# Retention then a sigmoid-gated FFN on Trainium2: the first token tile loaded and computed in natural layout instead of in halves of two chunks

## The chip, the cores and the metric

One Trainium2 chip, one core of it. The metric is the device time of one execution in microseconds (us); a kernel's time is the median of its runs. The inputs are float32 in device memory, the output is float32.

## What is computed

Recurrent retention over 4 batch entries, 8 heads, 768 tokens and head size 64, and then a gated feed-forward block on the 3072 resulting rows of 512:

```
gamma = 1 - 2 ** (-5 - arange(H))
for t in range(S):
    state = gamma * state + k[:, :, t] (outer) v[:, :, t]
    y[:, :, t] = q[:, :, t] @ state / sqrt(D)
x = y as [B * S, H * D]                      # 3072 x 512
out = (sigmoid(x @ w_gate) * (x @ w_val)) @ w_out   # d_ff = 1536
```

## The kernel before, in words

**Tiling.** The sequence is cut into six tiles of 128 tokens. A tile holds 128 tokens of all four batch entries, which is 512 rows of the FFN. The recurrence is done in its chunked form. Inside a chunk the scores k.q are multiplied by a decay or a causal mask (VectorE) and multiplied with v. What comes from earlier chunks goes through a running state `za`, of which `zb` is the bf16 copy. A tile is two "pairs" i, each of two batch entries j, so pairs 0 and 1 are tile 0, and pairs 2 to 11 are tiles 1 to 5.

**Tiles 1 to 5.** `load_kq` and `load_v` load a pair: k and q by DMAs that cast to bf16 (lines 63 and 67), v in float32 (line 57), all issued by GpSimd (POOL). `scale_v` (line 202) makes `vs`, v times a power of gamma from the table `tabs`, on POOL or on VectorE (DVE). k and q are transposed by TensorE (`transpose`, pairs 2 and 3) or by DMA transposes that SyncE (SP) issues (`xbar`, line 193, pairs 4 to 11). `block(old, new)` then runs the products: `scores` (line 210), `mask` (216), `inter` (226), `intra` (233), `y_out` (241), `state` (248), `state_sum` (257).

**The FFN.** `up(t, n1)` makes one of 12 slices of hidden units: four matmuls with the gate weights and four with the value weights (line 366), a sigmoid on ScalarE (ACT, line 376) and a product on DVE (line 377). `down` (line 393) multiplies with `w_out`, copies out of PSUM on ACT and stores through SP.

**Tile 0** has code of its own. k of pair 0 comes in float32 by two hardware queues (SP and ACT, `k0f`), v of pair 1 in float32 by SP (`v1f`, issued at lines 432-433). q, k of pair 1 and v of pair 0 come by casting DMAs on POOL. Here one batch entry of a pair lies on 64 partitions with two neighbouring tokens each (`k2`, `v2`), and q on 32 partitions with four (`q4`), so that the pieces in device memory are 512 or 1024 bytes long. `first_k`, `first_q`, `first_scores`, `first_y` and `first_state` work on half and quarter arrays (64x64). For the state of tile 0, POOL scales k of pair 0 (`k0s`) and v of pair 1 (`v1s`), line 342. `keep_on(n)` issues n matmuls of the identity (line 420) whose result nobody reads.

**What sets the order.** The program order of each engine is that of the code: `tc.manual_schedule()`. The `plan` at the end says behind which FFN group of tiles 1 to 4 each step of the recurrence stands. POOL's DMA issues share eight semaphores: the ninth waits until the first has landed, and so on.

Of the kernel before, what the change touches and what calls it, by code (L numbers as in the profile page):

```python
# [8 lines left out]
F32 = mybir.dt.float32  # L9
# [6 lines left out]
def kernel(  # L16
# [37 lines left out]
    def load_v(i):  # L54
        t, h = divmod(i, 2)
        vf[i] = ld.tile([C, 2 * H, D], F32, tag="vf", name="vf", bufs=4)
        nc.gpsimd.dma_start(out=vf[i], in_=v[2 * h:2 * h + 2, :, t * C:(t + 1) * C, :].rearrange("b h s d -> s (b h) d"))  # L57
# [33 lines left out]
    def first(t, x, b, n, part, eng):  # L91
        r = C // n
        eng.dma_start(out=t[part * r:(part + 1) * r].rearrange("p h j d -> p h (j d)"),
                      in_=x[b, :, 0:C, :].rearrange("h (p j) d -> p h (j d)", j=n))

    k0f = ld.tile([C, H, 2, D], F32, tag="vf", name="k0f", bufs=4)
    v1f = ld.tile([C, H, 2, D], F32, tag="vf", name="v1f", bufs=4)
    k2 = [ld.tile([C, H, 2, D], BF16, tag="kn", name="k2", bufs=6) for _ in range(2)]
    k0s = ld.tile([C, H, 2, D], BF16, tag="kn", name="k0s", bufs=6)
    q4 = at.tile([C, H, 4, D], BF16, tag="kqX", name="q4", bufs=4)  # L100
    v2 = [at.tile([C, H, 2, D], BF16, tag="vs", name="v2", bufs=4) for _ in range(2)]
    v1s = at.tile([C, H, 2, D], BF16, tag="vs", name="v1s", bufs=4)

    first(k0f, k, 0, 2, 0, nc.sync)
    first(k0f, k, 1, 2, 1, nc.scalar)
    nc.scalar.preload_act_table(AX.Exp)
    tok = const.tile([128, NT + 2], F32, name="tok")
    col = const.tile([128, C], F32, name="col")
    dist = const.tile([128, 2, C], F32, name="dist")
    nc.gpsimd.iota(tok[:, 0:NT], pattern=[[C, NT]], base=0, channel_multiplier=1, allow_small_or_imprecise_dtypes=True)  # L110
    nc.gpsimd.iota(col, pattern=[[1, C]], base=0, channel_multiplier=0, allow_small_or_imprecise_dtypes=True)
    nc.gpsimd.iota(dist, pattern=[[-1, 2], [1, C]], base=0, channel_multiplier=-2, allow_small_or_imprecise_dtypes=True)
    for b in range(B):
        first(q4, q, b, 4, b, nc.gpsimd)


    for b in range(2):
        first(k2[1], k, 2 + b, 2, b, nc.gpsimd)
    for b in range(2):
        first(v2[0], v, b, 2, b, nc.gpsimd)  # L120
    for s in range(2):
        load_gate_val(s)

    lgp = const.tile([128, NP], F32, name="lgp")
    lsc = const.tile([128, 1], F32, name="lsc")
    nlg = const.tile([128, H], F32, name="nlg")
    nc.vector.memset(lsc, math.log(scale))
    for h in range(H):
        nc.vector.memset(lgp[h % 2 * D:(h % 2 + 1) * D, h // 2:h // 2 + 1], lg[h])
    lsn = const.tile([128, NP], F32, name="lsn")  # L130
    nc.vector.tensor_scalar(lsn, lgp, float(C), math.log(scale), op0=ALU.mult, op1=ALU.add)
    ident = const.tile([128, 128], BF16, name="ident")
    causal = const.tile([128, 128], F32, name="causal")
    farther = const.tile([128, 2, C], F32, name="farther")
    nc.vector.tensor_scalar(ident, col, tok[:, 0:1], None, op0=ALU.is_equal)  # L135
    nc.vector.tensor_scalar(dist[D:128], dist[D:128], 2.0 * D, None, op0=ALU.add)
    nc.vector.scalar_tensor_tensor(farther, dist, -1.0e6, dist, op0=ALU.mult, op1=ALU.max)
    nc.vector.tensor_scalar(tok[:, NT:NT + 2], dist[:, :, 0], -1.0, None, op0=ALU.mult)
    for h in range(H):
        nc.vector.memset(nlg[:, h:h + 1], -lg[h])  # L140
    tabs = const.tile([128, H, NT + 2], F32, name="tabs")
    nc.vector.tensor_tensor(tabs, tok.unsqueeze(1).to_broadcast([128, H, NT + 2]),
# [7 lines left out]
    def make_taby1(p):  # L150
        nc.scalar.activation(taby[:, 1, p, :], col, AX.Exp, scale=lgp[:, p:p + 1], bias=lsn[:, p:p + 1])
# [425 lines left out]
```

## Time and profile before

| | us |
|---|---|
| runs of the kernel before | 240.84, 243.07, 243.61 |
| their median | 243.07 |
| the profiled execution | 243.72 |
| its span from first to last instruction | 242.0 |
| TensorE matmul busy | 223.2 (92%) |
| DVE / ACT / POOL busy | 109.2 / 80.0 / 101.6 |

The profile is of one execution. In its rows, a group of instructions has an engine, a line, the operation, what it writes and reads, how often it occurs, and in brackets how long the engine stood idle ahead of it and what ended that. "PE" is TensorE's matmuls, "PEld" its weight loads. The chain of waits follows the work that ended last back to the start. "PEclk" is the granted TensorE clock. In the rows of DMA queues, q0 is what POOL issues and q1 is what SP issues; a size of "128.0 KB" is that of what is written, which for a casting load is half of what is read.

### The profile page before, as it was taken

The page shows a single profiled execution, that of the slowest core. Times are in us where ns is not written, and L with a number is a line of the kernel's source. Part 1 is how long each engine was busy: PE and PEld are TensorE (multiplying, and loading weights), DVE is VectorE, ACT ScalarE, POOL GpSimd, SP SyncE. Part 2 cuts the span into 40 slices and gives each one's busy share as a digit, 9 for nine tenths or more (in the row PEclk, how much of TensorE's full clock was granted, in tenths as well). Part 3 has the DMA queues.
Part 4 walks back from the last instruction along what each step waited for, and adds up shares of the span by engine and source line. Part 5 has one row for each costly group of instructions (what it writes and reads, how often), then busy time and mean ns, then how long its engine had stood idle before and what let it go on. Part 6 is the DMA issues. An engine that isn't in the chain of part 4 may idle for free.

```text
span 242.0 us, 4687 instructions
## 1 busy us (share of the span) xinstructions
PE 223.2 (92%) x1925; PEld 124.4 (51%) x1948; DVE 109.2 (45%) x189; ACT 80.0 (33%) x133; POOL 101.6 (42%) x123
## 2 busy tenths in 40 slices
PE   2892999998959999999999999999999999999995
PEld 1761744454748885454454544544544544444444
DVE  3572145417289345575491454490634651243401
ACT  7543324332522421233332143231233222233211
POOL 8941985889997281399769420000000000000000
PEclk9999599999999999999999999999999999999999
DMA  7999799999999999999999974001150002200022
GB/s 132 183 199 185 87 176 176 215 175 193 249 147 133 98 125 139 106 265 106 180 98 175 253 141 90 0 0 75 58 131 3 0 0 89 88 0 0 3 85 88
DMA packets 77269, 28.09 MB, mean 116 GB/s; under 512 B 61888, under 2 KB 73024, under 8 KB 77248
## 3 DMA queue, kind: packets, MB, share of 16 engines
q0 software_dynamic: 54496, 16.26, 70.9%
q1 hardware_dynamic: 22080, 11.21, 27.6%
q10 hardware_dynamic: 672, 0.33, 0.5%
q8 instruction: 15, 0.25, 0.5%
q14 instruction: 6, 0.05, 0.1%
HBM read 28.31 MB, written 6.29 MB: 143 GB/s over the span
## 4 chain that ended last, share of the span: by engine, by line
PE 86%; DMA 6%; DVE 5%; issue 1%; ACT 0%; SPq 0%; DVEq 0%; ACTq 0%
PE ff L366 52%; PE ff L393 24%; DMA v1f<-in_v_dram 4%; DVE vs L202 2%; PE ff L233 2%; DMA k0f<-in_k_dram 2%; PE ff L210 2%; PE ff L226 1%; PE ff L406 1%; PE ff L248 1%; DVE qT L308 1%; DVE st L216 1%; PE ff L187 1%; PE ff L420 1%; PE ff L334 0%
## 5 line engine op out<-in xcount | busy, mean ns | idle before, releaser
L377 DVE TENSOR_TENSOR hT<-gs,ff 128x512 bf16<-128x512 f32 x72 | 49.0, 686 | 75.3 <-PE ff L366 71.8
L366 PE MATMUL ff<-xT,wg 128*128 128x512 bf16 (+1 forms) x338 | 74.5, 347 | 1.0 <-ACT xT L339 0.6
L366 PE MATMUL ff<-xT,wv 128*128 128x512 bf16 (+1 forms) x340 | 74.9, 350 | 0.1
L376 ACT ACTIVATE gs<-ff 128x512 f32<-128x512 f32 x72 | 42.9, 597 | 78.9 <-PE ff L366 76.7
L393 PE MATMUL ff<-wo,hT 128*128 128x512 bf16 x263 | 61.1, 379 | 0.9 <-issue 0.3
L366 PEld LDWEIGHTS <-wv 128*128 128x128 bf16 x344 | 34.4, 100 | 29.5 <-issue 0.2
L366 PEld LDWEIGHTS <-wg 128*128 128x128 bf16 x344 | 33.4, 99 | 28.7 <-issue 0.7
L393 PEld LDWEIGHTS <-hT 128*128 128x128 bf16 x276 | 26.2, 98 | 30.7
L397 ACT COPY ob<-ff 128x512 f32<-128x512 f32 x23 | 13.4, 585 | 49.3 <-PE ff L393 49.2
L216 DVE TENSOR_TENSOR st<-ff,causal 128x512 bf16<-128x512 f32 x40 | 24.7, 679 | 6.3 <-PE ff L210 6.3
L241 DVE TENSOR_TENSOR xT<-ff,taby 128x512 bf16<-128x512 f32 x20 | 12.9, 686 | 31.2 <-PE ff L233 31.2
L67 POOL DMA_DIRECT2D qn<-in_q_dram x20 | 15.2, 773 | 13.9 <-DMA qn<-in_q_dram 13.4
L202 POOL TENSOR_TENSOR vs<-vf,tabs 128x1024 bf16<-128x1024 f32 x8 | 15.7, 1960 | 4.0 <-DMA vf<-in_v_dram 3.6
L67 POOL DMA_DIRECT2D kn<-in_k_dram x20 | 15.2, 765 | 2.3 <-DMA kn<-in_k_dram 2.2
L57 POOL DMA_DIRECT2D vf<-in_v_dram x10 | 11.9, 1193 | 5.2 <-DMA qn<-in_q_dram 3.4
L261 ACT CAST zb<-za 128x512 bf16<-128x512 f32 x10 | 6.2, 616 | 13.4 <-DVE za L257 12.2
L63 POOL DMA_DIRECT2D kn<-in_k_dram x10 | 9.1, 910 | 1.3 <-DMA vf<-in_v_dram 1.3
L63 POOL DMA_DIRECT2D qn<-in_q_dram x10 | 9.1, 907 | 0.2 <-DMA kn<-in_k_dram 0.2
L420 PE MATMUL ff<-ident 128*128 128x128 bf16 x52 | 6.0, 290 | 2.0 <-DVE ident L135 2.0
L233 PE MATMUL ff<-st,vs 128*64 128x128 bf16 x160 | 6.6, 222 | 0.7 <-DVE vs L202 0.7
L248 PE MATMUL ff<-vs,kn 128*64 128x64 bf16 x128 | 3.6, 196 | 2.7 <-DVE vs L202 2.7
L420 PEld LDWEIGHTS <-ident 128*128 128x128 bf16 x52 | 4.6, 132 | 2.7 <-DVE ident L135 2.0
(74 smaller groups left out, 124.0 us busy)
## 6 DMA issues: line engine op xcount, KB each, us to landing
out_dram<-ob SPq DMA_DIRECT2D x23, 256.0 KB, 2.9
vf<-in_v_dram POOLq DMA_DIRECT2D x10, 512.0 KB, 8.6
wg<-in_moe_w_gate_dram POOLq DMA_DIRECT2D x6, 256.0 KB, 6.7
wv<-in_moe_w_val_dram POOLq DMA_DIRECT2D x6, 256.0 KB, 7.4
wo<-in_moe_w_out_dram POOLq DMA_DIRECT2D x4, 384.0 KB, 8.0
kn<-in_k_dram POOLq DMA_DIRECT2D x10, 128.0 KB, 8.3
kn<-in_k_dram POOLq DMA_DIRECT2D x20, 64.0 KB, 8.5
qn<-in_q_dram POOLq DMA_DIRECT2D x10, 128.0 KB, 9.3
```

The lines of the kernel that those rows point to most:

```text
L57: nc.gpsimd.dma_start(out=vf[i], in_=v[2 * h:2 * h + 2, :, t * C:(t + 1) * C, :].rearrange("b h s d -> s (b h) d"))
L63: nc.gpsimd.dma_start(out=tiles[i][:, 0:H], in_=src[0])
L67: nc.gpsimd.dma_start(out=dst[:, e], in_=pairs[:, 1 - e])
L202: eng.tensor_tensor(vs[i][:, j0 * H:(j0 + n) * H, :].rearrange("s (j h) d -> s j h d", j=n), vf[i][:, j0 * H:(j0 + n) * H, :].rearrange("s ...
L216: nc.vector.tensor_tensor(st[i, j], sc[i, j][e], causal4, op=ALU.mult)
L241: nc.vector.tensor_tensor(xT[t][:, :, c:c + C], y[i, j], taby[:, t], op=ALU.mult)
L366: nc.tensor.matmul(u[:, i * n:(i + 1) * n], w[:, kk, n1 * 128:(n1 + 1) * 128], xT[t][:, kk, lo:hi], start=(kk == 0), stop=(kk == KT - 1))
L376: nc.scalar.activation(g, ps[0], AX.Sigmoid)
L377: nc.vector.tensor_tensor(hT[t][:, n1s[0]:n1s[-1] + 1, lo:hi], g.rearrange("p (i n) -> p i n", n=n), ps[1].rearrange("p (i n) -> p i n", n ...
L393: nc.tensor.matmul(o, hT[t][:, n1, b * C:(b + 1) * C], wo[:, n1, :], start=(n1 == 0), stop=(n1 == NFF - 1))
L397: nc.scalar.copy(ob, o)
L420: nc.tensor.matmul(u[:, :128], ident, ident, start=True, stop=True)
```

## The change

Tile 0 is loaded and computed like the other tiles: 128 tokens on 128 partitions, one batch entry (a "half tile", `entry(t, j)`) after the other. k and q of the very first batch entry come in float32 by SP and ACT and are cast by DVE and ACT. All else of tile 0 comes by casting DMAs on POOL's queue, in the order k, q of entries 1, 2, 3 and then v of both pairs, with pieces of 256 bytes in device memory. v is not scaled for tile 0; the state is made from `ks`, k scaled by POOL in four half tiles (line 309 of the new file), and the decay table for tile 0 is over (token, token) of one entry. The tables that are needed later (`tabs`, `taby`, `causal`) are made behind the first scores. `up` of tile 0 starts with all 512 rows instead of two halves of 256. Further on, `vs` of pairs 2 and 3 is made by POOL instead of DVE, and a piece of `down(0, 3)` stands ahead of the products of pair 2 instead of behind.

```diff
-    k0f = ld.tile([C, H, 2, D], F32, tag="vf", name="k0f", bufs=4)
-    v1f = ld.tile([C, H, 2, D], F32, tag="vf", name="v1f", bufs=4)
...
-    first(k0f, k, 0, 2, 0, nc.sync)
-    first(k0f, k, 1, 2, 1, nc.scalar)
+    def first(dst, x, b, n, eng):
+        eng.dma_start(out=dst, in_=x[b:b + n, :, 0:C, :].rearrange("b h s d -> s (b h) d"))
...
+    first(kf, k, 0, 1, nc.sync)
+    first(qf, q, 0, 1, nc.scalar)
...
-    for b in range(B):
-        first(q4, q, b, 4, b, nc.gpsimd)
-    for b in range(2):
-        first(k2[1], k, 2 + b, 2, b, nc.gpsimd)
-    for b in range(2):
-        first(v2[0], v, b, 2, b, nc.gpsimd)
-    for s in range(2):
+    for b in range(1, B):
+        first(entry(kn[b // 2], b % 2), k, b, 1, nc.gpsimd)
+        first(entry(qn[b // 2], b % 2), q, b, 1, nc.gpsimd)
+    for i in range(2):
+        first(vs[i], v, 2 * i, 2, nc.gpsimd)
+    for s in range(3):
         load_gate_val(s)
...
+    def first_transposes(i, j, engs):
+        for which, (x, eng) in enumerate(zip((kn[i], qn[i]), engs)):
+            tp = bank([128, NP, C], BF16)
+            for p in range(NP):
+                nc.tensor.transpose(tp[:, p, :], heads(x, j, p), ident)
+            eng(kqT[i][:, which, j], tp)
+    def first_scores(i, j):
+        scores(i, j)
+        for e, st in enumerate((stA, stB)):
+            st[i, j] = at.tile([128, NP, C], BF16, tag=f"st{e}", name=f"st{e}", bufs=4)
+            nc.vector.tensor_tensor(st[i, j], sc[i, j][e], decay[:, e], op=ALU.mult)
+    def first_y(i, j, eng):
...
+        for p in range(NP):
+            for e, st in enumerate((stA, stB)):
+                nc.tensor.matmul(o[half(e), p, :], vs[i][:, j * H + 2 * p + e, :], st[i, j][:, p, :],
+                                 start=(p == 0), stop=True, skip_group_check=True)
+        c = (2 * i + j) * C
+        eng(xT[0][:, :, c:c + C], o)
+    def first_scaled(i, j, x):
+        nc.gpsimd.tensor_tensor(entry(ks[i], j), x, tabs[:, :, 0].unsqueeze(2).to_broadcast([C, H, D]), op=ALU.mult)
...
-    first_k(0, (2 * r, 2 * r + 1), nc.vector.tensor_copy)
-    keep_on(14)
-    first_q()
-    for b in range(2):
-        first(v1f, v, 2 + b, 2, b, nc.sync)
...
-    nc.scalar.copy(v2[1], v1f)
-    keep_on(8)
-    first_scaled(v1s, v1f)
...
+    keep_on(12)
+    first_transposes(0, 0, (dve, act))
+    keep_on(4)
+    first_scores(0, 0)
+    first_transposes(0, 1, (act, act))
+    later_constants()
+    keep_on(4)
+    first_scores(0, 1)
+    first_transposes(1, 0, (act, act))
+    keep_on(4)
+    first_scores(1, 0)
+    first_transposes(1, 1, (act, act))
+    nc.scalar.preload_act_table(AX.Sigmoid)
+    keep_on(4)
+    first_scores(1, 1)
+    keep_on(4)
+    first_y(0, 0, act)
+    first_y(0, 1, act)
+    keep_on(8)
+    first_y(1, 0, act)
+    first_y(1, 1, dve)
+    first_scaled(0, 0, kf)
+    first_scaled(0, 1, entry(kn[0], 1))
     load_gate_val(3)
+    first_scaled(1, 0, entry(kn[1], 0))
+    first_scaled(1, 1, entry(kn[1], 1))
     load_gate_val(4)
     load_gate_val(5)
-    gate0 = up_part(0, wg, (0, 1), 0, 256)
-    first_y(1)
-    val0 = up_part(0, wv, (0, 1), 0, 256)
...
+    for n1 in range(4):
         up(0, (n1,))
     first_state(0)
+    up(0, (4,))
+    first_state(1)
     up(0, (5,))
...
+    extend_taby(1)
     load_kq(2)
...
     load_next(3)
+    scale_v(2, nc.gpsimd)
...
-    scale_v(2, nc.vector, (0,))
-    scale_v(2, nc.vector, (1,))
     load_next(4)
+    down(0, 3, 0, 6)
     new_y(2)
...
-        1: [(0, transpose, 3, 1), (0, load_next, 5), (1, scaled_early, 3), (2, block, None, 3), (4, block, 3, None),
+        1: [(0, transpose, 3, 1), (0, scaled, 3), (0, load_next, 5), (2, block, None, 3), (4, block, 3, None),
```

Here `later_constants()` makes `lgp`, `tabs`, `taby` and `causal` on DVE and ACT.

How the order moves on the engines, at the places that matter. First POOL at the start of the program. `q_83`, `k_81` and `v_84` are the bf16 tiles in halves and quarters; `kn`, `qn` and `vs` are the natural ones; each row is one DMA, or as many as its x says.

```order
-L93 DMA q_83<-in_q_dram 32x8x256 x4
-L93 DMA k_81<-in_k_dram 64x8x128 x2
-L93 DMA v_84<-in_v_dram 64x8x128 x2
+L112 IOTA ahead 128x128
+L92 DMA kn<-in_k_dram 128x8x64
+L92 DMA qn<-in_q_dram 128x8x64
+L92 DMA kn<-in_k_dram 128x8x64
+L92 DMA qn<-in_q_dram 128x8x64
+L92 DMA kn<-in_k_dram 128x8x64
+L92 DMA qn<-in_q_dram 128x8x64
+L92 DMA vs<-in_v_dram 128x16x64 x2
```

There are eight DMAs on POOL's queue ahead of the weights as before, but they now bring all of v and not only half of it.

Second POOL between the weights. `k0s<-k0f` and `v1s<-v1f` scale for the state before; `ks` does now.

```order
 L79 DMA wv<-in_moe_w_val_dram 128x4x256
-L342 TENSOR_TENSOR k0s<-k0f,tabs 128x1024
+L309 TENSOR_TENSOR ks<-kf,tabs 128x512
+L309 TENSOR_TENSOR ks<-kn,tabs 128x512
 L79 DMA wg<-in_moe_w_gate_dram 128x4x256
 L79 DMA wv<-in_moe_w_val_dram 128x4x256
-L342 TENSOR_TENSOR v1s<-v1f,tabs 128x1024
+L309 TENSOR_TENSOR ks<-kn,tabs 128x512 x2
```

No instruction of POOL between the weight loads reads `v1f` any more.

Third POOL between the loads of pairs 3 to 5, the changed kernel alone: `vf` is v in float32, `vs` the scaled v, and `taby` a table.

```order
L57 DMA vf<-in_v_dram 128x16x64
L196 TENSOR_TENSOR vs<-vf,tabs 128x1024
L63 DMA kn<-in_k_dram 128x8x64
L67 DMA kn<-in_k_dram 128x4x64 x2
L63 DMA qn<-in_q_dram 128x8x64
L67 DMA qn<-in_q_dram 128x4x64 x2
L57 DMA vf<-in_v_dram 128x16x64
L159 TENSOR_TENSOR taby<-taby,gup 128x512
L196 TENSOR_TENSOR vs<-vf,tabs 128x1024
L63 DMA kn<-in_k_dram 128x8x64
```

The two rows of `vs` stand there anew: before, POOL went from one load to the next, and DVE did both.

179 lines of the change are left out of this document (54 added, 125 removed).

## The prediction

> **What bounds the kernel now.** I read the page first: TensorE is busy 92% of the span, and the chain of waits is its matmuls for 86%. What a change can win is time in which TensorE stands still or runs slowly.
>
> ```profile
> PE   2892999998959999999999999999999999999995
> PEclk9999599999999999999999999999999999999999
> DMA  7999799999999999999999974001150002200022
> PE 86%; DMA 6%; DVE 5%; issue 1%; ACT 0%; SPq 0%; DVEq 0%; ACTq 0%
> ```
>
> The gaps are in the first twelve slices of 6.05 us: slices 0, 1, 3 and 11 of PE, and one slice at half clock. The DMA engines are busy without a break until slice 23, so a second bound lies close behind. The chain of waits in order of time names the first gap, and the stage table sizes it:
>
> ```profile
> 0.75 5.39 DMA k0f<-in_k_dram
> ...
> 13.94 9.32 DMA v1f<-in_v_dram
> ...
> 23.36 1.05 ACT v L445
> ...
> 24.46 1.07 PE ff L334 x27
> ...
> 35.79 0.38 PE ff L351 x32
> ...
> 40.90 7.93 PE ff L366 x36
> 48.84 1.29 PE ff L393 x6
> ```
> ```profile
> 20.40:24.40 4.00, 0.00 (x0) 0.00 (x0) 0.00 (x0) 1.04 (x1) 0.97 (x1) 0.89 1.03 160
> 24.40:30.30 5.90, 5.84 (x55) 4.30 (x56) 0.69 (x1) 2.18 (x5) 5.79 (x11) 0.50 0.73 90
> 30.30:36.00 5.70, 5.65 (x58) 2.63 (x56) 2.17 (x4) 1.79 (x3) 5.12 (x11) 1.00 1.21 175
> ```
>
> (Columns: stretch and length, busy time of PE, PEld, DVE, ACT, POOL, the granted clock, DMA share, GB/s written.) v of pair 1 lands at 23.26, ACT casts it, and TensorE does nothing from 20.33 to 24.46, 4.13 us. Then its clock is 0.50 until 30.3: 5.84 us of work at half speed, of which 2.92 us are lost. The twelve groups of `up` of tile 0 end at 48.84. Two smaller gaps come from the scaling of v on DVE:
>
> ```profile
> 59.06 0.41 PE L233 MATMUL ff<-st,vs 128*64 128x128 bf16 x8 [0.55 <-DVE vs L202]
> 59.66 0.41 PE L233 MATMUL ff<-st,vs 128*64 128x128 bf16 x8 [0.19 <-DVE vs L202]
> 68.12 4.48 DVE L202 TENSOR_TENSOR vs<-vf,tabs 128x512 bf16<-128x512 f32 x2
> 72.66 0.32 PE L248 MATMUL ff<-vs,kn 128*64 128x64 bf16 x8 [2.70 <-DVE vs L202]
> ```
>
> That is 0.74 us at pair 2 and 2.70 us at pair 3. The sum below is made against the profiled execution, 243.72 us (span 242.0); it is 0.65 above the median of 243.07.
>
> **When tile 0's data lands after the change.** POOL's queue now carries 6 x 1024 + 2 x 2048 = 10240 casting pieces, 128 bytes written each, where the old pieces were 256 and 512 bytes written. Two stretches show what such pieces cost, alone on the queue and beside DMA transposes:
>
> ```profile
> q0 software_dynamic: 1965, 0.28, 224.3%
> ```
> ```profile
> q0 software_dynamic: 12145, 3.02, 124.7%
> q1 hardware_dynamic: 6494, 1.86, 61.3%
> ```
>
> The first is 47.0 to 48.8, 1965 pieces in 1.8 us, 1092 per us. The second is 64 to 102, 12145 in 38 us, 320 per us. The opening has no transposes, and its hardware queues only bring kf and qf (2048 pieces) early, so I take the first: 9.4 us for 10240 pieces. kf and qf have no row of their own: 2048 pieces are 1.9 us at the first rate and 6.4 at the second, or nothing where they run beside the casts. I take 2.5, near the first, which has the same piece size and no transposes. With a start at 2.1 the last v lands at 14.0, bounds 11.5 to 18. The issues fit in: six of 0.92 (the row of line 63 below) and two of 1.19 us from 1.46 on end at 9.4.
>
> ```profile
> L57 POOL DMA_DIRECT2D vf<-in_v_dram x10 | 11.9, 1193 | 5.2 <-DMA qn<-in_q_dram 3.4
> ```
>
> **The opening chain.** After kf has landed (the old k0f did 5.4 us after its issue at 0.75; I take 6.5) each half tile goes transposes, two copies, scores, two products with the decay.
>
> ```profile
> 7.97 1.67 PE L420 MATMUL ff<-ident 128*128 128x128 bf16 x14
> 11.73 0.85 PE L319 MATMUL ff<-qT,kT 64*64 64x128 bf16 x16 [0.24 <-ACT qT L310]
> ...
> 18.07 0.62 PE L420 MATMUL ff<-ident 128*128 128x128 bf16 x8
> ```
> ```profile
> L324 DVE TENSOR_TENSOR stf<-ff,decay 128x512 bf16<-128x512 f32 x8 | 5.0, 676 | 1.5 <-PE ff L319 1.5
> ...
> L298 ACT COPY kT<-ff 128x1024 bf16<-128x1024 bf16 x1 | 1.0, 1012 | 1.4 <-PE ff L297 1.4
> ```
>
> A 128-wide matmul takes 0.119 us early (1.67/14) and 0.078 late (0.62/8): TensorE starts slow. Eight transposes are 0.95 us, eight scores 0.45, two copies of 128x512 1.01, two products 1.35. The first scores then are at 8.8 and DVE is free at 10.7. `later_constants` stands ahead there, 0.74 (eight memsets) + 0.2 + 0.65 on DVE and then an exponential of 0.65 on ACT, so ACT is held until 12.9 with the copies of half tile 2 behind it. From there: copies to 14.0, scores 14.5, transposes of half tile 3 to 15.4, copies to 16.2, scores 16.7, products 18.1, y 0.45 and the last cast 0.69: `up` starts at **20.0**, six us behind v. Bounds 19.5 (no slack lost) and 21.5 (kf at 8). So v, which set the end before, does not any more; DVE's products do.
>
> **A: `up` of tile 0.** Twelve groups of eight 128x512 matmuls at full clock, with two first states:
>
> ```profile
> 32.17 1.03 PE L366 MATMUL ff<-xT,wg 128*128 128x512 bf16 x4
> ...
> 33.90 1.03 PE L366 MATMUL ff<-xT,wg 128*128 128x512 bf16 x4
> ```
>
> From start to start a group is 1.73 us (32.17 to 33.90): 20.8 us, plus 2 x 0.38 (chain, line 351). Weights don't hold it: at the 197 GB/s of the next row a 256 KB piece is 1.33 us, the twelve end at 30 to 32 us, and the last pair is needed at 37.
>
> ```profile
> 12.00:16.60 4.60, 4.17 (x65) 2.83 (x58) 3.55 (x7) 3.12 (x3) 2.99 (x3) 1.00 1.45 197
> ```
>
> For a slow clock at the start of `up` I add 1.7, the middle of 0 and 3.4 (half of a stretch as long as the 6.8 us seen). It ends at 20.0 + 20.8 + 0.8 + 1.7 = 43.3 instead of 48.84: **-5.5** (bounds -7.8 and -2.4).
>
> **B and C: scaling on POOL.** `vs` of pair 2 and of pair 3 leave DVE: -0.74 and -2.70 (bounds 0 each). POOL pays 2.0 us each, and 1.0 for a table made earlier:
>
> ```profile
> 23.43 1.91 POOL L342 TENSOR_TENSOR v1s<-v1f,tabs 128x1024 bf16<-128x1024 f32 x1 [8.44 <-DMA v1f<-in_v_dram]
> ...
> 40.52 1.19 POOL L57 DMA_DIRECT2D vf<-in_v_dram  x1 [0.79 <-issue]
> ...
> 56.28 0.92 POOL L63 DMA_DIRECT2D kn<-in_k_dram  x1
> ...
> 62.23 2.00 POOL L202 TENSOR_TENSOR vs<-vf,tabs 128x1024 bf16<-128x1024 f32 x1
> 64.11 0.93 POOL L63 DMA_DIRECT2D kn<-in_k_dram  x1
> ```
>
> POOL no longer waits 8.44 us for v1f, and needs 5 more. v of pair 2 was issued at 40.5 and landed 8.5 later, at 49.0:
>
> ```profile
> vf<-in_v_dram POOLq DMA_DIRECT2D x1, 512.0 KB, 8.5
> ```
>
> With the weights through by 31 it lands at 44.5 to 49 now, and 2.0 later its `vs` is ready, at 47 to 51; wanted at 54 (59.06 less A, and behind 1.3 of the moved piece). Load 4 (six us of issues, 56.28 to 62.2 is such a one), the table and 2.0 more bring pair 3's `vs` to 56 to 60; wanted at 63 (the state's first matmul stood at 69.6). The moved piece of `down(0, 3)` covers DVE's masks; it costs nothing, and 0.74 if it doesn't. But load 5, issued from 56.28 before, is now issued from 56 to 60, and load 6 (64.11) from 64 to 68: the lead that POOL had is spent.
>
> **D: what is late next.** A, B and C bring TensorE 9.0 us ahead, the loads of pair 6 hardly any. Its q is the closest:
>
> ```profile
> 84.97 3.26 SPq L193 DMA_TRANSPOSE kqX<-qn  x1
> ```
> ```profile
> kqX<-qn SPq DMA_TRANSPOSE x1, 17.0
> ```
> ```profile
> 102.09 0.04 issue
> 102.12 0.62 PE ff L210 x16
> ```
>
> It lands at 101.99, and the scores of pair 6 start at 102.12: no slack. Nine us ahead TensorE wants it at 93.1. The transposes of pairs 4 and 5 are no longer bunched with load 6, since SP issues them behind the last output of tile 0, which comes 6.2 us sooner (A and B); I expect the transposed q at 95.5 (91 if all of the six and more is kept, 101 if only POOL's issue counts), which gives back **+2.4** (0 to 8).
>
> Sum: 243.72 - 5.5 - 0.74 - 2.70 + 2.4 = 237.2; I say **237.1**.
>
> **The rivals.**
> 1. *All of it is kept*: the transposes come in time, D is 0, and 243.72 - 9.0 = 234.7. For it: six us less bunching. Against: no slack at all before.
> 2. *DMA takes it back*: load 6 as late as POOL's 68, D near 7.5, 242.2. For it: DMA engines at 9 through slice 22.
> 3. *A slow opening*: `up` at 23.5 and half clock for the whole 6.8 us, A about 0 and D 0: 240.0. For it: from 7 to 20 TensorE works in short bursts, with waits of up to 1.4 us between them (12.6 to 14.0). The Trainium skill (TensorE: Matmul & The Clock Gate, "What's actually happening") has the slow clock as the default, released after one busy window of about 3.4 us, and back after an idle one. The trace agrees with the second half: 0.50 follows 4.13 us of idling. Under the first, this opening stays slow until `up` itself has filled a window.
> 4. *Slower: the casting queue.* Should small pieces run at 320 per us beside kf and qf, v lands at 2.1 + 32 = 34.1, `up` runs from 35.4 to 58.7, A is +9.9, and with B and C 250.2. It decides from 400 pieces per us down: then `up` ends 3.4 us later than before and B and C are spent. Against it: the opening before had the same two kinds of queue, and k0f landed in 5.4 us. The Trainium skill (DMA: Bandwidth & Descriptors, "Specifications") asks for 512 B and more per transfer for full rate; the change goes from 512 and 1024 read to 256. The trace agrees in part: 0.28 MB in 1.8 us, 156 GB/s written, against 197.
>
> **How the numbers follow.** Forecast 0.45, rivals 1 to 4: 0.20, 0.13, 0.12, 0.10. One per cent, 2.4 us, is about what a measurement of this kernel can tell from no change, so faster is below 240.6: the forecast, rival 1, three quarters of rival 3 and a quarter of rival 2, 0.77; same 0.13; slower 0.10. The range: low from all good bounds, 243.72 - 7.8 - 3.44 = 232.5, less one for the spread of the runs: 231.5; high 242.5, which takes in rivals 2 and 3 and leaves out the fourth.
>
> **What would show it.** Right: no TensorE gap over 2 us between 20 and 43; `up` from about 20 to 43; no wait for `vs` at pairs 2 and 3; a wait for the transposed q of pair 6 of about 2 us near 93. Wrong: v landing behind 20; a clock of 0.50 beyond 27; `vs` of pair 3 behind TensorE; a wait at pair 6 over 5 us, or several at the pairs after.

## The result, and the profile after

The changed kernel takes 233.98 us in the median of four runs (230.83, 232.14, 235.82, 237.23), the kernel before beside it 242.77 (240.84 to 243.61). The ratio is 0.9546, 95% interval [0.9437, 0.9654]: faster, by some 9 us in the medians, 3 more than forecast and inside the range. The ratios here and below are of the runs within 1.5% of the fastest of their kernel, the medians of all runs, so the two need not give the same gain. The profiled run is the quickest, 230.83 us with a span of 229.0, and lies just below the low end of the range (231.5); the span of before was 242.0, so the two profiles have 13.0 us to account for, 4 more than the medians.

The page of after, its rows 2 (PE, PEclk) and its chain of waits by engine:

```profile
PE   4688999999999999999999999999999999999994
PEclk9979999999999999999999999999999999999999
PE 92%; ACT 2%; DMA 2%; DVE 1%; issue 1%; DVEq 0%
```

The gaps of slices 3 and 11 are gone, and the slow clock has moved from slice 4, where `up` ran, to slice 2, ahead of `up`. The chain in order of time (start, length, what) has no v in it any more:

```profile
0.75 3.90 DMA qf<-in_q_dram
...
10.19 0.72 ACT taby L155
10.92 0.97 ACT kqT L289 x2
...
17.12 0.70 DVE xT L306
...
34.02 5.78 PE ff L331 x26
39.79 1.29 PE ff L358 x6
...
53.42 1.75 PE ff L331 x16
...
60.03 3.60 PE ff L331 x32
```

`up` of tile 0 ends at 39.79 instead of 48.84: **9.05 us** of the 13.0. The next stage, down of tile 0 with pair 2, took from 48.84 to 63.47 before and takes from 39.79 to 53.42 now: 1.0 less. Pair 3 with its state took from 63.47 to 72.97 and takes from 53.42 to 60.03: 2.9 less. What follows is 169.03 us long before and 168.97 now. The stages of the opening (columns as in the prediction's table):

```profile
11.90:15.30 3.40, 3.07 (x32) 2.32 (x31) 1.73 (x3) 2.17 (x3) 3.40 (x5) 0.50 1.74 175
...
17.96:39.80 21.84, 21.68 (x126) 9.99 (x130) 8.77 (x13) 8.19 (x14) 17.31 (x30) 1.00 1.53 192
```

Half clock comes between 11.9 and 15.3, before `up`. (It also holds until about 8, where no clock was recorded yet: four transposes take 0.61 to 0.63 us up to there, and 0.39 to 0.40 between 9.3 and 9.9.) `up` is busy for 21.68 of 21.84 us at a clock of 1.00. TensorE's waits over the whole span are small, and none is for a scaled v or a transposed q:

```profile
PE ff L204 <- ACT kqT L289: 2.7, 4, 1.8
...
PE ff L331 <- DVE xT L306: 0.9, 1, 0.9
```

POOL's queue (start, length) is where the prediction had it: pair 2's `vs` from 45.27, pair 3's from 54.09, load 5 from 55.97.

```profile
45.27 1.93 POOL L196 TENSOR_TENSOR vs<-vf,tabs 128x1024 bf16<-128x1024 f32 x1 [0.96 <-DMA vf<-in_v_dram]
...
54.09 1.99 POOL L196 TENSOR_TENSOR vs<-vf,tabs 128x1024 bf16<-128x1024 f32 x1
55.97 0.94 POOL L63 DMA_DIRECT2D kn<-in_k_dram  x1
```

The transposed q of pair 6 is not. SP's queue, the transfers issued between 74 and 76 (the last column is the time to landing), and TensorE's use of it:

```profile
74.40 1.25 SPq L187 DMA_TRANSPOSE kqX<-qn  x1
```
```profile
kqX<-qn SPq DMA_TRANSPOSE x1, 5.3
```
```profile
89.08 0.62 PE L204 MATMUL ff<-kqX 64*128 64x128 bf16 x16
```

It lands at 79.7 and is used at 89.1: 9.4 us of slack, where the prediction had 95.5 against 93.1.

### The profile page after: what moved, and what is told of

It is laid out like the page before. It is cut to its first block, busy times and chain, and to the rows that moved or that the text cites. A ratio compares the mean times of both kernels' runs of the same rounds, so it can differ in the third digit from the quotient of the medians.

```text
span 229.0 us, 4355 instructions
## 1 busy us (share of the span) xinstructions
PE 217.6 (95%) x1770; PEld 119.5 (52%) x1792; DVE 102.4 (45%) x179; ACT 76.5 (33%) x127; POOL 108.7 (47%) x128
## 4 chain that ended last, share of the span: by engine, by line
PE 92%; ACT 2%; DMA 2%; DVE 1%; issue 1%; DVEq 0%
PE ff L331 55%; PE ff L358 26%; PE ff L204 3%; PE ff L227 2%; DMA qf<-in_q_dram 2%; PE ff L220 2%; PE ff L371 1%; ACT kqT L289 1%; PE ff L242 1%; PE ff L181 1%; PE ff L288 1%; PE ff L303 1%; PE ff L385 0%; PE ff L317 0%; DVE st L295 0%
## 5 line engine op out<-in xcount | busy, mean ns | idle before, releaser
L331 PE MATMUL ff<-xT,wg 128*128 128x512 bf16 (+1 forms) x331 | 73.7, 348 | 1.3 <-DVE xT L306 0.9
L331 PE MATMUL ff<-xT,wv 128*128 128x512 bf16 (+1 forms) x331 | 73.3, 348 | 0.2
L331 PEld LDWEIGHTS <-wv 128*128 128x128 bf16 x336 | 32.9, 98 | 29.4
L331 PEld LDWEIGHTS <-wg 128*128 128x128 bf16 x336 | 32.1, 98 | 29.3 <-issue 1.0
L235 DVE TENSOR_TENSOR xT<-ff,taby 128x512 bf16<-128x512 f32 x20 | 12.9, 686 | 32.9 <-PE ff L227 32.9
L196 POOL TENSOR_TENSOR vs<-vf,tabs 128x1024 bf16<-128x1024 f32 x10 | 19.8, 1983 | 9.4 <-PE ff L227 8.4
L295 DVE TENSOR_TENSOR st<-ff,decay 128x512 bf16<-128x512 f32 x8 | 5.1, 685 | 3.6 <-PE ff L204 3.6
L385 PE MATMUL ff<-ident 128*128 128x128 bf16 x40 | 5.0, 284 | 1.6 <-DVE ident L137 1.6
L204 PE MATMUL ff<-kqT 64*128 64x128 bf16 x64 | 3.5, 248 | 2.7 <-ACT kqT L289 2.7
```

The source lines that it names most:

```text
L196: eng.tensor_tensor(vs[i][:, j0 * H:(j0 + n) * H, :].rearrange("s (j h) d -> s j h d", j=n), vf[i][:, j0 * H:(j0 + n) * H, :].rearrange("s ...
L235: nc.vector.tensor_tensor(xT[t][:, :, c:c + C], y[i, j], taby[:, t], op=ALU.mult)
L331: nc.tensor.matmul(u[:, i * n:(i + 1) * n], w[:, kk, n1 * 128:(n1 + 1) * 128], xT[t][:, kk, lo:hi], start=(kk == 0), stop=(kk == KT - 1))
```

## The experiments

Two questions were open: where the 9.05 us of A come from, and whether the transposes of pair 6 (D) are free or were lucky. The first group starts from the kernel before, the second from the changed one. All times in one table; "down" is the start of the first `down` matmul, which is the end of `up` of tile 0 and can be compared between the two layouts; the last two columns are the landing of pair 6's q and TensorE's wait for it, all from the one profiled run of each.

| kernel | median, us | ratio to before on the same chip | `down` starts | q of pair 6 lands | wait |
|---|---|---|---|---|---|
| before | 242.77 | | 48.67 | 102.0 | 0 |
| e1 v early | 240.67 | 0.9986 [0.9907, 1.0065] | 44.39 | 92.6 | 0 |
| e2 scaling | 239.17 | 0.9944 [0.9900, 0.9988] | 46.92 | 96.1 | 1.1 |
| e8 both | 236.20 | 0.9831 [0.9707, 0.9955] | 45.05 | 99.2 | 4.8 |
| changed | 233.98 | 0.9546 [0.9437, 0.9654] | 39.63 | 79.7 | 0 |
| e9 changed, again | 231.45 | 0.9657 [0.9545, 0.9769] | 40.36 | 81.1 | 0 |
| e3 scaling undone | 233.60 | 0.9698 [0.9632, 0.9764] | 41.39 | 90.4 | 0 |
| e4 transposes held | 234.56 | 0.9745 [0.9687, 0.9803] | 40.99 | 91.7 | 1.3 |
| e5 constants later | 231.98 | 0.9694 [0.9577, 0.9812] | 41.98 | 92.8 | 1.4 |
| e6 no fillers | 232.44 | 0.9700 [0.9607, 0.9794] | 41.09 | 90.6 | 0 |
| e7 halves | 233.95 | 0.9763 [0.9646, 0.9879] | 42.16 | 88.7 | 0 |
| e10 load 5 held | 232.44 | 0.9674 [0.9599, 0.9749] | 40.39 | 86.6 | 0 |
| e11 wait for all | 237.02 | 0.9872 [0.9810, 0.9934] | 43.63 | 95.3 | 2.3 |
| e12 k, q of 6 first | 232.08 | 0.9666 [0.9629, 0.9703] | 40.98 | 83.2 | 0 |

The table also shows how far one profile can be trusted. Six kernels have the changed opening unaltered (changed, e9, e3, e4, e10, e12). In them `up` starts between 17.96 and 19.71 and `down` between 39.63 and 41.39; the profile of the changed kernel is the earliest of the six. Before and e2 share the old opening and lie 1.75 apart: behind the gap, three groups of eight matmuls run at half speed in before (1.76 to 1.91 us each), and one in e2 (1.88). So the 9.05 us of A stand between a late profile of the old opening and an early one of the new; over all these profiles the difference is 5.5 to 9.0, and a step of less than 1.8 us at `down` is not told apart by one pair of profiles.

### e1: the kernel before, with v of pair 1 issued at the start

```diff
     first(k0f, k, 1, 2, 1, nc.scalar)
+    for b in range(2):
+        first(v1f, v, 2 + b, 2, b, nc.sync)
...
-    nc.vector.memset(v1f[:, 0, 0, 0:1], 0.0)
-    for b in range(2):
-        first(v1f, v, 2 + b, 2, b, nc.sync)
```

> The kernel before, with one edit: v1f is issued right behind k0f on SP instead of behind the first scores. Theory (the wait for v1f and the half clock after it were the largest part of the gain): TensorE's 4.13 us gap and the 2.9 us at half clock go, up of tile 0 ends near 41.5 instead of 48.84, POOL is no longer held 8.4 us, and the time falls by about 7 us, to 236. Rival (it is the natural layout that matters, an earlier v1f only takes bandwidth from q and the weights): k0f or q land later, up starts later than 19.3 by about as much as is won, time within 2 us of before.

The time did not move, 0.9986 [0.9907, 1.0065], as the rival said. The 4.1 us wait for v is gone, and `down` starts 4.3 us sooner; but of that 1.9 was left at the end of the span (240.1 against 242.0). The waits of TensorE, then DVE's and POOL's queues at pair 3:

```profile
PE ff L250 <- DVE vs L204: 3.5, 2, 2.4
PE ff L307 <- DMA q<-in_q_dram: 2.2, 1, 2.2
```
```profile
63.84 5.33 DVE L204 TENSOR_TENSOR vs<-vf,tabs 128x512 bf16<-128x512 f32 x2
```
```profile
65.17 1.99 POOL L204 TENSOR_TENSOR vs<-vf,tabs 128x1024 bf16<-128x1024 f32 x1
67.06 1.55 POOL L167 TENSOR_TENSOR taby<-taby,gup 128x512 f32<-128x512 f32 x1
```

q's last entry lands 2.9 us later (11.69 instead of 8.79), with v loaded beside it now, and TensorE waits 2.2 for it. At pair 3 the two products on DVE take 5.33 us in place of the 1.28 that they take alone, while POOL multiplies beside them. From the first `down` to the state of pair 3 the stage is 0.9 us longer than before, and behind this wait the clock falls to 0.51 from 70.4 to 73.9, which makes the rest some 1.6 longer: that is where the rest of the 4.3 went. So v's gate was worth 4.3 at `down` against the profile of before (2.5 against e2, which has the same gate), but not the rest of A, and a gain of TensorE runs into the next wait.

### e2: the kernel before, with the scaling alone

```diff
+    scale_v(2, nc.gpsimd)
     new_kqT(2)
...
-    scale_v(2, nc.vector, (0,))
-    scale_v(2, nc.vector, (1,))
     load_next(4)
+    down(0, 3, 0, 6)
...
-        1: [(0, transpose, 3, 1), (0, load_next, 5), (1, scaled_early, 3), (2, block, None, 3), (4, block, 3, None),
+        1: [(0, transpose, 3, 1), (0, scaled, 3), (0, load_next, 5), (2, block, None, 3), (4, block, 3, None),
```

> The kernel before, with the scaling of v of pairs 2 and 3 moved from DVE to POOL and the piece of down(0,3) moved ahead, nothing else of the change. Theory (B and C add up by themselves): no wait of TensorE for vs, 3.4 to 3.9 us faster, about 239. Rival (POOL pays 4 us, its loads come later, and the transposed q of pair 6 has no slack): TensorE waits 2 to 5 us for pair 6 near 100, and the time is within 1.5 us of before or slower.

The ratio is 0.9944 [0.9900, 0.9988], about 1.3 us where B and C are 3.4. The waits for `vs` are gone, but one for a transposed q is there, and the wait for v is as it was:

```profile
PE ff L334 <- ACT v L445: 5.2, 1, 5.2
...
PE ff L210 <- DMA kqX<-qn: 1.1, 1, 1.1
```

q of pair 6 lands at 96.1, when TensorE already stands before it. In the profile the stages of B and C, from the first `down` to the last state matmul of pair 3, are 20.2 us after 24.1, and all that follows is 1.1 longer than before: D is there in the old opening, at some 1 us. That the median moved by less than the 2.8 left of the two is not explained by one profile.

### e3: the changed kernel, with the scaling of pairs 2 and 3 back on DVE

```diff
-    scale_v(2, nc.gpsimd)
...
+    scale_v(2, nc.vector, (0,))
+    scale_v(2, nc.vector, (1,))
     load_next(4)
...
-        1: [(0, transpose, 3, 1), (0, scaled, 3), (0, load_next, 5), (2, block, None, 3), (4, block, 3, None),
+        1: [(0, transpose, 3, 1), (0, load_next, 5), (1, scaled_early, 3), (2, block, None, 3), (4, block, 3, None),
```

> The changed kernel, with the scaling of v of pairs 2 and 3 back on DVE. Theory: the waits for vs come back, 2.7 us at pair 3's state above all, and the time is 3 to 4 us more than the changed kernel's, about 237 to 238. Rival (the 3.9 us product on DVE was an accident of the crowded stage in the kernel before, not of DVE as such): DVE's products take 0.68 us each, no wait, time within 1 us of the changed kernel's.

In the time it is not told apart from the changed kernel, and it costs less than B and C were: the stage of pair 3 (from the transposes of its first half to the last state matmul) is 8.2 us, against 7.0 in the changed kernel and 9.9 before. TensorE's wait, DVE's products and POOL's around them:

```profile
PE ff L242 <- DVE vs L196: 0.9, 2, 0.7
```
```profile
61.34 1.28 DVE L196 TENSOR_TENSOR vs<-vf,tabs 128x512 bf16<-128x512 f32 x2
```
```profile
56.79 2.04 POOL L196 TENSOR_TENSOR vs<-vf,tabs 128x1024 bf16<-128x1024 f32 x1
...
64.62 2.03 POOL L196 TENSOR_TENSOR vs<-vf,tabs 128x1024 bf16<-128x1024 f32 x1
```

The two products take 1.28 again: no POOL product runs beside them here (POOL's end at 58.83 and start at 64.62). In e1 and before, POOL multiplies just then, and single products take 3.89 and 3.88 us. POOL in the kernel before, where the two products on DVE go from 68.12 to 72.60:

```profile
70.04 2.00 POOL L202 TENSOR_TENSOR vs<-vf,tabs 128x1024 bf16<-128x1024 f32 x1
71.93 1.56 POOL L165 TENSOR_TENSOR taby<-taby,gup 128x512 f32<-128x512 f32 x1
```

The long product begins at 68.72 and ends 0.56 us after POOL's first one. In e1 the two end 0.56 and 0.55 after POOL's products. DVE's other products beside a POOL product, all with one operand in PSUM, take at most 0.71 in before, e1 and the changed kernel. The Trainium skill (GPSIMD Engine Reference, "Key points") says that GpSimd shares its SBUF interfaces with VectorE, with contention for VectorE instructions with two SBUF inputs. These products have two SBUF inputs, and the traces agree: 0.68 us without, 3.9 with a POOL product beside them. Why DVE stands 1.3 us longer than POOL's product, from before its start, the traces don't show. So most of C was such a meeting (the stage is 1.7 us shorter without it, and 2.9 in the changed kernel), and either a shift of the two queues or the move to POOL ends it.

### e4: the changed kernel, with pair 4's transposes held back

```diff
         kqT[i] = at.tile([128, 2, 2, NP, C], BF16, tag="kqX", name="kqX", bufs=4)
+        if i == 4:
+            nc.vector.memset(kqT[i][:, 0, 0, 0, 0:1], 0.0)
```

> The changed kernel, with the DMA transposes of pair 4 held back by a one-column write of DVE behind block 3, so that they are issued near 65 (54 in the changed kernel, 64 in the kernel before) beside the loads of pair 6. Theory (transposes and loads bunched together slow each other, which is what stage 64 to 102 of the kernel before shows): from issue to landing the transposes take 10 to 17 us instead of 6 to 8, the transposed q of pair 6 lands behind 90, and TensorE waits 1 to 8 us for it; time 1 to 8 us above the changed kernel's. Rival (the slow stage of the kernel before had another cause): transposes still take 6 to 8 us each, TensorE does not wait, time within 1 us.

The memset holds SP's first transpose until 67.1 instead of 54.3. The six transposes take 4.2 to 11.8 us, with the medians of the stage from 67 to 92 as follows, and the q of pair 6 lands at 91.7:

```profile
kqX<-kn SPq DMA_TRANSPOSE x3, 9.0
kqX<-qn SPq DMA_TRANSPOSE x3, 8.1
```

TensorE waits 1.3 us for it. That is slower than the 5.9 and 7.7 of the changed kernel and far from the 15.0 and 15.3 of before, so bunching alone does not make the old figures. Nor does this run show that holding them back costs anything: in e5, which holds nothing, the six take 8.1 to 13.2 us.

### e5: the changed kernel, with the later constants behind the last transposes

```diff
     first_transposes(0, 1, (act, act))
-    later_constants()
...
     first_transposes(1, 1, (act, act))
+    later_constants()
```

> The changed kernel with its later constants (eight small memsets, three products and two exponentials) built behind the transposes of the last half tile instead of behind the second's. Theory (the opening is a chain through ScalarE, which the two exponentials hold until 10.92): TensorE's 1.81 us of waiting at 11.93 goes, the first up starts at about 16.3 to 16.8 in a profile with the same clock (17.96 in the changed kernel's; the last v lands at 14.08 and bounds it), and the time is 1 to 1.6 us below the changed kernel's on this chip. Rival (the loads bound it: the last v at 14.08, then two products, a copy and the first up): the wait only moves to the v, the first up starts at 17.3 to 18 and the time is the changed kernel's within 0.5 us.

No gain: 231.98 beside 231.45 for e9. The first `up` starts at 18.62 (e9: 18.69). The longest wait for ScalarE's copies is 0.7 us (1.8 in the changed kernel, 1.0 in e9), but TensorE waits 1.0 for DVE's products in its place, since the constants now stand ahead of the last two of these. The time is what the rival said, for another reason than the landing of v. In this execution the half clock also falls into `up` (the stretch's clock is 0.60):

```profile
18.62:22.90 4.28, 4.22 (x12) 1.60 (x13) 0.69 (x1) 0.60 (x1) 4.28 (x6) 0.60 1.46 195
```

### e6: the changed kernel without its fillers

```diff
     first_transposes(0, 0, (dve, act))
-    keep_on(4)
     first_scores(0, 0)
...
     first_y(0, 1, act)
-    keep_on(8)
     first_y(1, 0, act)
```

(All six of those behind the first twelve matmuls.)

> The changed kernel without its filler products between the opening's steps (32 of 44 left out; the first 12 stay). Theory (A came out larger than predicted partly since TensorE was at the full clock when the first up began, and the fillers keep it busy enough for that): the clock stays or falls to half beyond 18 us, the first up's first 3 to 7 us run at half speed, and up of tile 0 ends 1.5 to 3.5 us later (43.3 at the latest), the time 1.5 to 3.5 us above the changed kernel's. Rival (the opening's own products are work enough, and the fillers lie on TensorE's path themselves): up ends where it did, within 0.5 us, or up to 1 us earlier.

`down` starts at 41.09 against 40.36 in e9, 0.7 later, less than expected and within what the unaltered opening shows. TensorE's queue as `up` begins:

```profile
17.79 0.58 PE L331 MATMUL ff<-xT,wg 128*128 128x512 bf16 x1 [0.88 <-DVE xT L306]
18.59 1.06 PE L331 MATMUL ff<-xT,wg 128*128 128x512 bf16 x2 [0.22 <-issue]
19.45 1.85 PE L331 MATMUL ff<-xT,wv 128*128 128x512 bf16 x4
21.14 1.03 PE L331 MATMUL ff<-xT,wg 128*128 128x512 bf16 x4
```

Four matmuls last 1.85 us until 21.1 and 1.03 from then on: `up` starts 0.9 us sooner than in e9, but runs at half speed for its first 3.3 us and takes 23.3 us where it took 21.7, which loses 1.6. That the fillers lay on TensorE's path and so cost the 0.9 is likely and not shown, for the start of the unaltered opening varies by more. In sum this run shows no gain of the fillers that is clear of the spread. This is the half clock of the prediction's third rival, without its late start. The Trainium skill (TensorE: Matmul & The Clock Gate, "What's actually happening") has the slow clock released after one busy window of about 3.4 us; the trace agrees, with 3.3 us of `up` before the change of speed.

### e7: the changed kernel, with k and q of chunk 0 loaded in halves of 64 partitions

```diff
-    first(kf, k, 0, 1, nc.sync)
-    first(qf, q, 0, 1, nc.scalar)
+    for r in range(2):
+        s = slice(64 * r, 64 * r + 64)
+        for dst, x in ((kf, k), (qf, q)):
+            (nc.sync, nc.scalar)[r].dma_start(out=dst[s], in_=x[0, :, s, :].rearrange("h s d -> s h d"))
```

> The changed kernel with chunk 0's k and q loaded as the kernel before loaded its k: each in two halves of 64 partitions, one on SP and one on ScalarE, the bytes on each queue the same as now. Theory (the halves made k's first load of the kernel before land at 4.83 and 6.14; whole loads on 128 partitions are quicker): kf and qf are both complete at 5.5 to 6.5 instead of 4.2 and 4.7, the first up starts 0.5 to 1.5 us later (18.5 to 19.5 where TensorE's clock is full from 9 to 12 us on), and the time is 0.5 to 1.5 us above the changed kernel's. Rival (the bytes and their order on the two queues set it; or the transposes of chunk 0 are not on the path that sets the first up): kf and qf are complete within 0.5 us of now, or later without a move of the first up, and the time is unchanged within 0.5 us.

The theory was wrong for k, which is complete at 4.11 (4.15 whole), and too mild for q, at 6.71 (4.65). Transfers issued in the first 2 us, with their time to landing:

```profile
kf<-in_k_dram SPq DMA_DIRECT2D x1, 128.0 KB, 3.4
kf<-in_k_dram ACTq DMA_DIRECT2D x1, 128.0 KB, 2.7
...
qf<-in_q_dram ACTq DMA_DIRECT2D x1, 128.0 KB, 4.4
qf<-in_q_dram SPq DMA_DIRECT2D x1, 128.0 KB, 5.2
```
```profile
PE ff L290 <- ACT qn L146: 2.2, 1, 2.2
```

q's halves stand behind k's on both queues, and the same 512 KB take 2 us longer to land. The first `up` starts at 20.49, 1.8 after e9's and 0.8 after the latest of the unaltered openings, and the constants end 2.0 later (13.03, e9 11.04), so the landing of qf is on the path, almost one for one; the median is 1.5 to 1.9 above those of e10 and e12 on the same chip.

### e8: the kernel before with both, e1 and e2

> The kernel before, with its halves of two chunks and its layout kept, but both known waits taken away: v of entries 2 and 3 issued right behind k (no gate), and the products v times decay of pairs 2 and 3 on POOL, with the piece of down moved as the change does. Theory (the layout itself brought the rest: k and q of one chunk land at 4.2 to 4.7 and the first up starts at 18 instead of 21.7): up of tile 0 ends near 44.5, B and C come on top, no wait of TensorE on a product of v, and the time is about 236 to 238 on a chip where the kernel before takes 240 to 242: 2 to 4 us short of the changed kernel. Rival (the layout is neutral; the gate on v and the placing of the scaling were all of it): within 1 us of the changed kernel.

The edits are those of e1 and e2 together. Its profiled run was the longest of its four (243.35) and is read for its opening alone. The other three are 234.92 to 237.11, and the changed kernel's four on the same chip 231.10 to 232.39, so it is some 4 us short of it, and `down` starts at 45.05 against 40.36. In the profile TensorE also waited for the transposed q of pair 6:

```profile
99.33 0.82 PE L212 MATMUL ff<-kqX 64*128 64x128 bf16 x16 [4.76 <-DMA kqX<-qn]
```

By the two ratios, 0.9831 and 0.9657, taking away the two known waits is about half of the result. The layout of the first tile, with its loads and its order, is the other half. The two intervals reach 1.1 to 1.2% to either side, so the halves are rough.

### e9: the changed kernel again

> The changed kernel unaltered, for its time on the same chip as the other three and for a second profile. Theory (the profiled 230.83 is at the quick end of what the opening gives: the clock's first step falls where it may): the first up starts anywhere from 18.0 to 19.8, and the time is 232 to 235, its profile's span longer by what the start is later. Rival (the spread of 230.8 to 237.2 comes from somewhere else, such as the transfers of 54 to 90 us): the same start and a longer stage behind it.

The four runs are 231.10 to 232.39; the first `up` is at 18.69 and the span 229.8, so 0.7 later at the start and 0.8 longer in all. The theory holds for this pair. No profile of the changed kernel shows a run of 236 us, so what made two of the first four that long stays open.

### e10: the changed kernel, with load 5 held until pair 4's transposes have landed

```diff
+    def behind(i):
+        nc.gpsimd.tensor_copy(const.tile([128, 2], F32, name="seen"), kqT[i][:, :, 1, NP - 1, C - 1])
...
-        1: [(0, transpose, 3, 1), (0, scaled, 3), (0, load_next, 5), (2, block, None, 3), (4, block, 3, None),
-            (4, scaled, 4), (4, xbar, 4), (5, casts, 3), (5, load_next, 6), (7, scaled, 5), (7, xbar, 5),
+        1: [(0, transpose, 3, 1), (0, scaled, 3), (0, xbar, 4), (0, behind, 4), (0, load_next, 5), (2, block, None, 3), (4, block, 3, None),
+            (4, scaled, 4), (5, casts, 3), (5, load_next, 6), (7, scaled, 5), (7, xbar, 5),
```

> The changed kernel with the load of pair 5 held on POOL until both DMA transposes of pair 4 have landed (POOL copies two elements of them first), so these two run beside no casting load but the end of load 4; loads 5 and 6 and the transposes of pairs 5 and 6 come some 8 us later. Theory (the transposes are slow because casting loads run beside them: 5.3 to 8.5 us in the quick stages, 9 to 17 in the others): pair 4's transposes take 3 to 5 us each, while those of pairs 5 and 6, which still run beside loads, take 6 to 13; pair 6's q lands at 88 to 94, and TensorE waits 0 to 4 us for it, so the time is 0 to 4 us above the changed kernel's. Rival (the transposes set their own time): pair 4's take 6 to 9 us as now.

Pair 4's transposes, issued from 54.5 to 62:

```profile
kqX<-kn SPq DMA_TRANSPOSE x1, 5.5
kqX<-qn SPq DMA_TRANSPOSE x1, 4.4
```

4.4 us for q, with little but k's transposes and the end of load 4 beside it, against 8.5 in the changed kernel, 6.9 in e9 and 11.8 in e5. Those of pairs 5 and 6, with loads beside them, take 5.4 to 7.9. k's transpose is hardly quicker than in the changed kernel and e9 (5.9 and 5.7). So q's figure fits the theory that casting loads slow the transposes, on one profile, and by less than the quick and the other profiles differ; the time is unchanged, since no wait hung on it.

### e11: the changed kernel, with the last half tile transposed first

```diff
     keep_on(12)
+    first_transposes(1, 1, (act, act))
     first_transposes(0, 0, (dve, act))
...
-    first_transposes(1, 1, (act, act))
```

> The changed kernel with the transposes of its last half tile put first on TensorE: nothing of the first tile starts before the last k and q have landed at 10.4, as in the kernel before, where the transposes of q waited for all four entries. Loads, products and layout stay. Theory (the larger part of what the change gained beyond v is that natural layout lets each entry start as it lands): TensorE waits from about 7 to 10.8, its 12 us of opening work have only 7 us of loads to lie beside, and the first up starts at 20 to 21.7 (18.0 to 18.7 with a like clock now); the time is 2 to 3 us above the changed kernel's. Rival (the last v, at 14.1 to 14.9, bounds the opening whatever comes before it): the first up starts within 0.7 us of where it did.

`up` starts at 21.95 and `down` at 43.63, 3.3 after e9's and 2.2 to 4.0 after the six unaltered openings. The median, 237.02, is 4.6 and 4.9 us above e10 and e12 on the same chip (2.3 of it a wait for pair 6's q in the profile), and the ratio is 0.9872 against 0.9546 and 0.9657. The first wait, and TensorE's work by stage:

```profile
PE ff L288 <- DMA kn<-in_k_dram: 6.4, 1, 6.4
```
```profile
6.50:10.40 3.90, 0.70 (x6) 0.44 (x7) 0.00 (x0) 0.28 (x1) 3.90 (x5) 1.00 2.24 143
10.40:21.95 11.55, 8.72 (x120) 7.00 (x121) 8.30 (x21) 7.42 (x13) 9.43 (x12) 1.00 1.66 183
```

From 6.5 to 10.4 TensorE is busy for 0.70 us (e9: 3.35), and 11.55 us of opening remain behind the last load. The loads land when they did; only the work beside them is gone.

### e12: the changed kernel, with k and q of pair 6 ahead of the scaling of pair 4

```diff
-            (4, scaled, 4), (4, xbar, 4), (5, casts, 3), (5, load_next, 6), (7, scaled, 5), (7, xbar, 5),
+            (4, load_kq, 6), (4, scaled, 4), (4, xbar, 4), (5, casts, 3), (5, load_v, 6), (7, scaled, 5), (7, xbar, 5),
```

> The changed kernel with the k and q loads of pair 6 ahead of the scaling of pair 4 on POOL (v of pair 6 stays behind it): a version that may beat it. Theory (where the stage of transposes is slow, TensorE waits about 1.3 us for pair 6's q, as in two of the kernels of before): k and q of pair 6 are issued near 62 instead of 63.8, pair 6's q lands 1 to 2 us sooner after its issue time of now, no wait of TensorE on a transpose, and the time is the changed kernel's or up to 1.3 us below it. Rival (more casting loads at once beside the transposes of pair 4 make these slower, which uses up the head start): the same wait or a larger one, and the time unchanged or up to 2 us above.

232.08, its four runs from 231.49 to 232.17; no wait for a transpose, pair 6's q at 83.2. It is not told apart from the changed kernel (231.45 and 233.98 on other chips). No version here is shown to beat it.

## Why the prediction was right, and where it was not

**Landing of v: right.** The forecast was 14.0 from the rate of 1092 pieces per us. The two loads of v land 5.6 and 6.1 us after their issues at 6.8 and 7.9, the last at 14.08. In the stretch from 7.5 to 9, 1793 pieces in 1.5 us are 1195 per us, near the rate that was taken:

```profile
q0 software_dynamic: 1793, 0.23, 236.6%
```

Rival 4, the queue at 320 pieces per us, did not happen, and v does not set the end of the opening.

**A: the right mechanism, mis-sized by 3.6 us.** `up` started at 17.96, not 20.0 (and below the bound of 19.5), and paid nothing for a slow clock instead of 1.7; its own length was right (21.83 against 20.8 + 0.8). In this profile the 2.04 at the start come of one step, "after kf has landed (the old k0f did 5.4 us after its issue at 0.75; I take 6.5)". kf and qf landed at 4.15 and 4.65. k0f was 512 KB on the two queues before TensorE could start; kf is 256 KB on one, and qf 256 KB on the other. The sum of the bytes is the same; in e7, as halves of 64 partitions like k0f's, they take until 6.71. e7 also gives the price of such an error: 2 us on qf's landing became 1.8 of `up`. ScalarE was accordingly free of the constants at 10.92 instead of 12.9; from there to `up` 7.04 us passed, and 7.1 were forecast.

The other 1.7 was a mean over a chance. In all six unaltered openings `up` takes 21.7 us to the first `down`, at full clock; e5 has the half clock inside (19.5 to 22.9), e6 shows its price at 1.6 us. The bound of nothing was the true one for `up`, but the opening ahead of it pays. In e3, e4 and e12 the first sixteen products of `y` take 1.06 us, and 0.64 in the changed kernel; from the constants to `up` it is 8.2 to 8.3 us there, and `up` starts at 19.3 to 19.7. So rival 3 was half right: the opening can stay slow to its end, at a price of 1.2 to 1.3 us, and `up` itself then runs at full clock. Part of the 3.6 is thus luck of this execution: against the latest of the six profiles the miss at the start is 0.3, and the 8.8 us between the medians leave about 5 for A and D together, once B and C have taken 3.9.

What the prediction didn't see is why `up` starts so much sooner. It named the gap of 4.13 us and the slow clock behind it. e1 took exactly these away and won 4.3 of the 9 us at `down`; e8 shows nearly the same (45.05). Most of the other 4.7 come of starting each half tile as its own k and q land: e11, which keeps layout, loads and products and gives up only that, loses 2.2 to 4.0 and starts `up` at 21.95, where e1 does at 21.65. What remains, about 1, is the length of `up`: 22.7 us in e1 and 21.7 in the changed kernel, for the old order has products of `y` (0.6) and a wait of 0.2 in it.

**B and C: right**, -1.0 and -2.9 for -0.74 and -2.70. The forecast knew the price and not the cause. 3.88 us for one product was a meeting of DVE with POOL; e3, where they don't meet, waits 0.9 with the scaling on DVE. (B's 1.0 and C's 2.9 are lengths of stages, the forecasts were waits.)

Of the prediction's own signs, no gap of TensorE over 2 us between 20 and 43, no wait for `vs` and no half clock beyond 27 were there; the wait of 2 us near 93 was not.

**POOL's dates: right, to 0.3 us.** Pair 2's `vs` is ready at 47.2 (47 to 51), pair 3's at 56.1 (56 to 60), loads 5 and 6 are issued from 55.97 and 63.79 (56 to 60, 64 to 68).

**D: wrong in this profile.** The step that failed is "I expect the transposed q at 95.5". It let the transposes of pair 6 keep most of their old time of 17.0 us; they took 5.9 and 5.3. TensorE wanted q at 89.1, not 93.1, and it had been there for 9 us. So the case that came true is rival 1, with a larger A: 243.72 - 9.05 - 1.0 - 2.9 - 0.06 = 230.7 for the profiled 230.83.

The other profiles show that D varies from one to the next. Pair 6's q lands anywhere from 79.7 to 92.8 in the versions whose `down` starts before 42.2 us, and TensorE waits for it in two of nine (e4, whose transposes were held, 1.3 us; e5, 1.4). The quick and the slow stage carry nearly the same packets; the first rows are the changed kernel from 54 to 80, the second e5 from 57 to 93:

```profile
q0 software_dynamic: 13520, 3.21, 124.2%
q1 hardware_dynamic: 6487, 1.85, 48.0%
```
```profile
q0 software_dynamic: 13687, 3.26, 125.9%
q1 hardware_dynamic: 6671, 2.17, 55.0%
```

Shares times 16 engines times 26 and 36 us, divided by the packets, are 38 and 53 ns for a casting packet, 31 and 47 for one of the hardware queue. Each packet of either kind takes 40 to 50% longer. Load 5 is issued at nearly the same time in both (55.97 and 55.08), but the first transpose is not: 54.32 and 56.96. In the quick profiles of the changed kernel and e9 (54.86 against 55.55) it goes out ahead of load 5. In e5, e6 and e7, where `down` starts later, it goes out behind it (56.96, 55.59 and 56.72 against 55.08, 55.17 and 55.10), and q lands at 88.7 to 92.8. That is a lead and not a cause shown: e12, with another order of loads, has its first transpose behind load 5 too (55.69, 54.86) and lands q at 83.2. If it holds, D hangs on how early the opening ends. Whether D explains the runs of 235.82 and 237.23, which left no profile, stays open.

## What to carry to other kernels

Lay out the first tile so that each load brings something that can start by itself: about a third of the gain at `down` (2.2 to 4.0 of 9 us by e11) was not a wait taken away but work put beside loads. Size the first loads by what the first step needs of them, and ask of every operation that is oddly slow in one place which other engine was running there. Where a transfer has no slack in one profile, look at several executions before pricing it: its time here ran from 5 to 13 us in the versions with the new opening. The same goes for an opening: six profiles of the same one differ by 1.8 us, so a single pair of profiles settles no smaller step.

## What the runs showed of the hardware beyond that

A DVE product of 128x512 with two inputs in SBUF takes 0.68 us alone. Beside a POOL product it took 3.88 (before), 3.89 and 1.52 us (e1), and ended 0.55 to 0.56 us after POOL's each time. POOL pays a little too: its product for `taby` takes 1.55 and 1.56 us in these two places, and 1.03 to 1.13 elsewhere.

The granted clock reads 1.00 in a stretch for which no record was taken: e6's stage from 17.79 to 21.10 shows it while seven matmuls need 3.09 us, against fifteen in 3.26 in e9 from 18.69. Matmul times tell the clock there, the column doesn't.

```profile
17.79:21.10 3.31, 3.09 (x7) 1.13 (x9) 0.00 (x0) 0.60 (x1) 3.31 (x5) 1.00 1.45 197
```
```profile
18.69:22.00 3.31, 3.26 (x15) 1.54 (x17) 0.69 (x1) 1.12 (x2) 3.27 (x5) 1.00 1.46 195
```
